# A spectral block beside a gated feed-forward: the sixteen-point stages as 64x64 matmuls, filter loads on GpSimd's queue, roots moved up

## The chip, the core and the metric

The kernel runs on one core of a Trainium2 chip. The metric is the time of one execution on the device in microseconds; the time before is the median of three runs. A profiled execution gives the trace: what each engine (TensorE, VectorE, ScalarE, GpSimd, and SyncE, which issues DMAs) did, and what it waited for. PE in the profile is TensorE, PEld its weight loads, DVE VectorE, ACT ScalarE, POOL GpSimd, SP SyncE, and SPq the queue on which SyncE issues DMAs.

## What is computed

The input is 2048 rows of 640 values in bf16. Cut to what matters, the reference is:

```python
xn = _layernorm(x, axis=-1)                      # 2048 x 640
X  = jnp.fft.rfft2(xn, axes=(-2, -1))            # 2048 x 321 complex
s  = jnp.fft.irfft2(X * (w_r + 1j * w_i), s=(S, D), axes=(-2, -1))
g  = _silu((_gelu(xn @ w_gate) * (xn @ w_up)) @ w_down)   # 640 -> 1536 -> 640
return x + s * g
```

So two independent branches start from the normalized input: a two-dimensional Fourier filter, and a feed-forward part with two input matrices of 640 x 1536 and one output matrix of 1536 x 640. Their product is added to the input.

## The kernel before

**Tiling.** The 2048 rows are 16 slabs of 128 rows (row = 16 n2 + n1, a slab is one n1). The feed-forward part works on four groups g of four slabs, 512 rows each: for each of 12 tiles t of the hidden dimension five matmuls into `psg` and five into `psu` (L634), GELU on ScalarE into `ge` (L638), the product into `uT` on VectorE (L640), then the down matmuls (L650) and the gate (`gate_out`).

**The Fourier branch.** The transform over 2048 rows is split into 128 x 16. Stage 1 (`slab_S1`, `slab_D`) does the 128-point part and the transform over the 640 columns, slab by slab, and stores the result in the DRAM scratch `ZDR`. After all 16 slabs `load_B2` reads it back with the 16-point direction on partitions: partition = (real or imaginary, n1, a), with 32 further row indices h in the free dimension (`B2`, 128 x 32 x 321). The sixteen-point stage `pair_S2(h)` handles two of these 32 indices: two matmuls of 128 x 128 by 128 x 321 with the weights `MG` into `px`, a copy to `xs` on ScalarE, and two products `p1`, `p2` with the filters `W1`, `W2` on VectorE. `pair_S2i(h)` is the inverse: four matmuls with `N1`, `N2` into `pu`, a copy to `us`, and two stores into the DRAM scratch `UDR`. The filter's partitions hold pairs of 16-point sets, so that `MG`, `N1` and `N2` are 128 x 128 with zeros where the sets don't mix (the mask `mk`, L333). Then `load_V` reads `UDR`, `vfold`, `slab_S1i` and `slab_Di` make the output of the branch, and `multiply_add` joins it with the gate and stores.

**The order.** Nothing is scheduled by a planner. The list `back` holds 144 slots of feed-forward work in order, one slot being five matmuls of 512 columns, ten of 256, or eight down matmuls (1.08 to 1.09 us each). `put(s, ...)` attaches other work to slot s, and the build issues each slot's feed-forward work and then its attached items. Each engine executes its own instructions in that order, so an instruction that waits holds up all that is behind it on its engine. Group 0 of the feed-forward part ends at slot 35, group 1 at 71, group 2 at 107.

**Where the touched steps stand.** The filter loads (`w_plus`, `w_minus`, `w_dup`) are issued by SyncE, one item behind each early `slab_D`; `w_edge` halves two columns on GpSimd at slots 50 and 53. The tables for the 16-point stage are made by `mg_iota`, `mg_phase` (GpSimd, slot 14), `mg_wrap` (VectorE, slot 20), `mg_sin` (ScalarE, slot 22), `mg_build` (58) and `mg_turn` (61). Statistics of a slab (`stats`) are followed, some slots later, by the inverse square roots of a group (`rsqrt4_a`, `rsqrt4_b`, which end in `nb`), then by `norm` on VectorE and `norm_act` on ScalarE (L430). `tfwd(1)`, slot 27, fills the second half of the table `Tfwd` on ScalarE (L232). `load_B2` is at slot 58. The pairs run from slot 66:

```python
    sb = z_end + 8
    for h in range(NS):
        down = back[sb][0] is down_third
        put(sb, pair_S2, h)
        if h > 0:
            put(sb + (0 if down else 1), pair_S2i, h - 1)
        sb += 1 if down else 2
    put(sb, pair_S2i, NS - 1)
    put(sb, load_V)
    vs0 = sb + 9
```

This gives slots 66 to 92, `load_V` at 92 and the first `slab_S1i` at 101. PSUM is split into two banks each for `psg` and `psu`, and two buffers of two banks each (`psB`) for all the rest, `px` and `pu` among it.

Of the kernel before, what the change touches and what calls it, by code (L numbers as in the profile page):

```python
# [14 lines left out]
P = 128  # L15
# [60 lines left out]
def build(nc, env):  # L76
# [26 lines left out]

    def w_plus(i, lo):
        WT, sp = spw[i]
        for ri in range(2):
            p0 = ri * 64 + lo * 16
            nc.sync.dma_start(out=WT[p0:p0 + 16, :, :], in_=sp[:, lo * 32:lo * 32 + 32, :])

    def w_minus(i, lo):  # L110
        WT, sp = spw[i]
        if lo == 0:
            nc.sync.dma_start(out=WT[32:48, :, :], in_=sp[:, 96:64:-1, :])
        else:
            nc.sync.dma_start(out=WT[48:64, 1:NH, :], in_=sp[:, 127:96:-1, :])
            nc.sync.dma_start(out=WT[48:64, 0, :], in_=sp[:, 64, :])

    def w_dup(i):
        WT = spw[i][0]
        nc.sync.dma_start(out=WT[96:128, :, :], in_=WT[32:64, :, :])  # L120
# [10 lines left out]
    MG = consts.tile([P, 2, P], BF16)  # L131
# [87 lines left out]
    def tinv_row():  # L219
        row = consts.tile([1, P], BF16)  # L220
        nc.gpsimd.memset(row[:, 0:P:2], 1.0)
        nc.gpsimd.memset(row[:, 1:P:2], -1.0)
        nc.sync.dma_start(out=Tinv[64:65], in_=row.unsqueeze(1).to_broadcast([1, NS, P]))
# [56 lines left out]
    def mg_iota():  # L280
        kr = mtile([2, 2, 2, 16], INT32, "kr")
        lc = mtile([2, 2, 2, 16], INT32, "lc")
        for ri in range(2):
            nc.gpsimd.iota(kr[:, ri, 0], pattern=[[0, 2], [1, 16]], base=0, channel_multiplier=0)
            nc.gpsimd.iota(kr[:, ri, 1], pattern=[[0, 2], [-1, 16]], base=15, channel_multiplier=0)
            nc.gpsimd.iota(lc[:, ri, 0], pattern=[[1, 2], [0, 16]], base=0, channel_multiplier=0)
            nc.gpsimd.iota(lc[:, ri, 1], pattern=[[-1, 2], [0, 16]], base=1, channel_multiplier=0)
        mg["kr"], mg["lc"] = kr, lc

    def mg_phase():  # L290
        n1_f, z_f = bits("mb", [(2, 15), (1, 1)])
        mg["z"] = z_f
        kr = mg["kr"]

        def aff(name, src, a, b):
            t = c1(name)
            nc.gpsimd.tensor_scalar(out=t, in0=src, scalar1=float(a), scalar2=b, op0=ALU.mult, op1=ALU.add)
            return t

        n1x = aff("n1x", n1_f, 128.0, 0.0)  # L300
        zc = aff("zc", z_f, -512.0, 512.0 + 1024.0)
        php0 = aff("php0", hi_f, 512.0, zc)
        php1 = aff("php1", php0, 1.0, 512.0)
        phm0 = aff("phm0", hi_f, -512.0, zc)
        phm1 = aff("phm1", phm0, 1.0, 1536.0)
        phs0 = aff("phs0", hi_f, 512.0, 1536.0)
        phs1 = aff("phs1", phs0, 1.0, 512.0)
        phs2 = aff("phs2", n1_f, 64.0, phs0)
        phs3 = aff("phs3", phs2, 1.0, 512.0)
        vg = mtile([2, 2, 2, 16], INT32, "vg")  # L310
        vs = mtile([4, 16], INT32, "vs")
        for ri, pm, ph in ((0, 0, php0), (1, 0, php1), (0, 1, phm0), (1, 1, phm1)):
            nc.gpsimd.tensor_scalar(out=vg[:, ri, pm], in0=kr[:, ri, pm], scalar1=n1x, scalar2=ph,
                                    op0=ALU.mult, op1=ALU.add)
        for j, ph in enumerate((phs0, phs1, phs2, phs3)):
            nc.gpsimd.tensor_scalar(out=vs[:, j, :], in0=kr[:, 0, 0, 0, :], scalar1=n1x, scalar2=ph,
                                    op0=ALU.mult, op1=ALU.add)
        mg["vgf"], mg["vs"] = vg.rearrange("p a b c d -> p (a b c d)"), vs
# [5 lines left out]
    def mg_sin():  # L324
        mg["sg"] = sg = mtile([P], FP32, "sg")
        mg["ss"] = ss = mtile([4, 16], FP32, "ss")
        nc.scalar.activation(out=sg, in_=mg["vgf"], func=ACT.Sin, bias=negpi, scale=TWO_PI / 2048.0)
        nc.scalar.activation(out=ss, in_=mg["vs"], func=ACT.Sin, bias=negpi, scale=TWO_PI / 2048.0)

    def mg_build():  # L330
        sg, ss, z_f, lo_f = mg["sg"], mg["ss"], mg["z"], lo_b
        mk = mg["kr"].rearrange("p a b c d -> p (a b c d)").bitcast(FP32)
        nc.vector.tensor_scalar(out=mk, in0=mg["lc"].rearrange("p a b c d -> p (a b c d)"), scalar1=lo_f,  # L333
                                scalar2=None, op0=ALU.is_equal)
        nc.vector.tensor_tensor(out=MG[:, 1, :], in0=sg, in1=mk, op=ALU.mult)
        nc.vector.tensor_copy(out=MG[:, 0, :], in_=MG[:, 1, :])
        lo0 = affine("lo0", lo_f, -1.0, 1.0)
        mz1 = c1("mz1")
        nc.vector.tensor_tensor(out=mz1, in0=z_f, in1=lo0, op=ALU.mult)
        mz0 = c1("mz0")  # L340
        nc.vector.tensor_tensor(out=mz0, in0=lo0, in1=mz1, op=ALU.subtract)
        for ri in range(2):
            for pm, mz in ((0, mz0), (1, mz1)):
                q0 = ri * 64 + pm * 32 + pm * 16
                nc.vector.tensor_scalar(out=MG[:, 0, q0:q0 + 16], in0=ss[:, pm * 2 + ri, :], scalar1=mz,
                                        scalar2=None, op0=ALU.mult)
        mg["MJ"] = MJ = mtile([2, P], BF16, "MJ")
        nc.vector.tensor_copy(out=MJ[:, :, 0:64], in_=MG[:, :, 64:128])
        nc.vector.tensor_scalar_mul(out=MJ[:, :, 64:128], in0=MG[:, :, 0:64], scalar1=-1.0)

    def mg_turn():
        MJ = mg["MJ"]
        pt = psB.tile([P, 4, P], BF16, tag="b")
        for k in range(2):
            nc.tensor.transpose(out=pt[:, k, :], in_=MG[:, k, :], identity=ident)
            nc.tensor.transpose(out=pt[:, 2 + k, :], in_=MJ[:, k, :], identity=ident)
# [160 lines left out]
    def load_B2():  # L517
        B2 = big.tile([P, NH, L], BF16, tag="sB", name="B2")
        zv = ZDR.rearrange("c n (a h) l -> (c n a) h l", a=4)
        for q in range(4):  # L520
            nc.sync.dma_start(out=B2[:, 8 * q:8 * q + 8, :], in_=zv[:, 8 * q:8 * q + 8, :])
        st_b["B2"] = B2

    def pair_S2(h):
        B2 = st_b["B2"]
        px = psB.tile([P, 2, 512], FP32, tag="b")
        for k in range(2):
            hi = 2 * h + k
            nc.tensor.matmul(px[:, k, 0:L], lhsT=MG[:, min(hi, 1), :], rhs=B2[:, hi, :], start=True, stop=True)  # L529
        xs = work.tile([P, 2 * L], BF16, tag="m1", bufs=2)  # L530
        nc.scalar.copy(out=xs.rearrange("p (k l) -> p k l", k=2), in_=px[:, :, 0:L])  # L531
        p1 = work.tile([P, 2 * L], BF16, tag="p1", bufs=2)
        p2 = work.tile([P, 2 * L], BF16, tag="p2", bufs=2)
        for pp, WT in ((p1, W1), (p2, W2)):
            nc.vector.tensor_tensor(out=pp, in0=xs, in1=WT[:, 2 * h:2 * h + 2, :].rearrange("p k l -> p (k l)"),  # L535
                                    op=ALU.mult)
        st_b[h] = (p1, p2)

    uv = UDR.rearrange("n (a h) f -> (n a) h f", a=4)

    def pair_S2i(h):
        p1, p2 = st_b.pop(h)
        pu = psB.tile([P, 2, 512], FP32, tag="b")
        for NM, pp, first in ((N1, p1, True), (N2, p2, False)):
            for k in range(2):
                hi = 2 * h + k
                nc.tensor.matmul(pu[:, k, 0:L], lhsT=NM[:, min(hi, 1), :], rhs=pp[:, k * L:(k + 1) * L],  # L547
                                 start=first, stop=not first)
        us = work.tile([P, 2, L], BF16, tag="m2", bufs=3)
        nc.scalar.copy(out=us, in_=pu[:, :, 0:L])  # L550
        nc.sync.dma_start(out=uv[:, 2 * h:2 * h + 2, 0:L], in_=us[0:64, :, :])
        nc.sync.dma_start(out=uv[:, 2 * h:2 * h + 2, L:D], in_=us[64:128, :, 1:320])
# [3 lines left out]
    def load_V():  # L556
        V = big.tile([P, NS, D], BF16, tag="sB", name="Vin")
        for g in range(4):
            nc.sync.dma_start(out=V[:, 4 * g:4 * g + 4, :],
                              in_=UDR.rearrange("n p f -> p n f")[:, 4 * g:4 * g + 4, :])  # L560
# [30 lines left out]
    def slab_Di(n1):  # L591
        py = psB.tile([P, 2, 512], FP32, tag="b")
        d_matmuls(py, st_c.pop(n1))
        eo = work.tile([P, 2, LP], BF16, tag="p1", bufs=2)
# [32 lines left out]
    def ffn_piece(g, t, k, c0, c1_):  # L627
# [8 lines left out]
        if k == 0:  # L636
            cur["ge"] = work.tile([P, 512], BF16, tag="ge", bufs=3, name="ge")[:, c0:c1_]
            nc.scalar.activation(out=cur["ge"], in_=ps, func=ACT.Gelu_apprx_tanh)  # L638
        else:
            nc.vector.tensor_tensor(out=uT[g][:, t, c0:c1_], in0=ps, in1=cur["ge"], op=ALU.mult)  # L640

    def ffn_part(g, t, h):
        for k in range(2):
            ffn_piece(g, t, k, h * 256, h * 256 + 256)

# [87 lines left out]
    for g, st, rs, nf in ((1, (9, 10, 11, 12), 13, ((14, 15), (16, 17))), (2, (18, 20, 22, 24), 26, ((27, 28), (30, 32))),  # L733
                          (3, (33, 35, 37, 39), 40, ((41, 42), (45, 46)))):
# [18 lines left out]
    for n1, item in enumerate(filt):  # L753
        put([sl for sl, it in f_units.items() if it == (slab_D, n1)][0], *item)
    put(50, w_edge, 0)
    put(53, w_edge, 1)
    put(2, vt_iota, 1)
    put(12, tinv_angle, 1)
# [12 lines left out]
    for h in range(NS):  # L771
        down = back[sb][0] is down_third
        put(sb, pair_S2, h)
        if h > 0:
            put(sb + (0 if down else 1), pair_S2i, h - 1)
        sb += 1 if down else 2
    put(sb, pair_S2i, NS - 1)
    put(sb, load_V)
    vs0 = sb + 9
# [35 lines left out]
    for s, b in enumerate(back):  # L815
        b[0](*b[1:])
        for it in plan[s]:
            it[0](*it[1:])
    assert len(left) == 0
# [30 lines left out]
```

## Time and profile before

| | |
|---|---|
| median of 3 runs (lowest to highest) | 218.66 us (217.79 to 218.76) |
| the profiled execution's own time | 218.46 us |
| its span (first to last instruction) | 216.3 us |
| instructions | 4227 |
| TensorE busy | 203.4 us, 94% of the span |
| VectorE, ScalarE, GpSimd busy | 144.0, 129.3, 14.4 us |
| DMA moved | 31.77 MB in 35253 packets |

Lines in the profile read as follows. A group of instructions: line, engine, operation, output <- inputs, shape, count | busy us in all, mean ns of one | idle us of the engine just before them and what ended it. A wait: who <- for whom, us in all, times, longest. A piece of the chain: start us, length us, engine and what. A row of the timeline: start us, length us, engine, line, operation, what, and in brackets the idle time just before it and what ended it. Matmuls are pipelined: one's length in the profile is longer than the distance to the next one's start. All times are of one execution, counted from the span's start.

### The profile page before, as it was taken

Reading aid. Unit: us, or ns where it says so; the run is one execution under the profiler, and the core shown is the slowest. Engines: PE = TensorE matmul, PEld = TensorE weight load, DVE = VectorE, ACT = ScalarE, POOL = GpSimd, SP = SyncE. Lnnn points to the kernel's source line nnn. Section 1 sums busy time; section 2 is a strip of 40 time slices with the busy share of each in tenths; the row PEclk is TensorE's granted clock in tenths of the full one; section 3 lists DMA queues with packets and bytes.
Section 4 is the critical chain, followed back from the end, with each engine's and each line's share of the span. In section 5 each row is a group of like instructions: output and inputs, shape, how many; then the busy total and the mean of one; then the engine's idle time right before and its main releaser. Section 6 shows DMA issues by size and latency. Waiting matters only on the chain.

```text
span 216.3 us, 4227 instructions
## 1 busy us (share of the span) xinstructions
PE 203.4 (94%) x1504; PEld 131.8 (61%) x1504; DVE 144.0 (67%) x478; ACT 129.3 (60%) x215; POOL 14.4 (7%) x44
## 2 busy tenths in 40 slices
PE   0699999998999999999999999999999999999993
PEld 0389984676665555567665555557676656666773
DVE  8888988956987852352665544543667888894442
ACT  7556567594764945533785656651467666765721
POOL 8000203800000000000000000000000000000000
PEclk9999999999999999999999999999999999999999
DMA  5999999999999996329542222233943433322131
GB/s 163 344 363 361 340 161 105 142 149 134 128 203 212 159 210 112 75 62 334 185 91 62 62 58 48 47 79 102 371 150 95 120 121 100 112 66 64 28 108 50
DMA packets 35253, 31.77 MB, mean 147 GB/s; under 512 B 10336, under 2 KB 34016, under 8 KB 35040
## 3 DMA queue, kind: packets, MB, share of 16 engines
q1 hardware_dynamic: 35232, 31.50, 64.1%
q8 instruction: 12, 0.20, 0.4%
q14 instruction: 9, 0.07, 0.1%
HBM read 20.34 MB, written 7.87 MB: 130 GB/s over the span
## 4 chain that ended last, share of the span: by engine, by line
PE 81%; DVE 6%; ACT 5%; DMA 5%; issue 1%; SPq 0%; ACTq 0%; DVEq 0%
PE psg L634 22%; PE psu L634 22%; PE psg L650 9%; PE psu L650 9%; PE pu L547 4%; PE pv L583 2%; PE py L503 2%; PE py L502 2%; PE px L529 2%; DMA Vin<-UDR 2%; PE pd L502 2%; PE pd L503 2%; PE pz L494 2%; DMA UDR<-us 2%; PE pw L273 1%
## 5 line engine op out<-in xcount | busy, mean ns | idle before, releaser
L634 PE MATMUL psg<-xnT,Wg 128*128 128x512 bf16 (+1 forms) x275 | 61.4, 354 | 0.0
L634 PE MATMUL psu<-xnT,Wu 128*128 128x512 bf16 (+1 forms) x275 | 60.9, 352 | 0.0
L650 PEld LDWEIGHTS <-uT 128*128 128x128 bf16 x396 | 37.5, 98 | 13.7 <-DVE uT L640 0.2
L640 DVE TENSOR_TENSOR uT<-psu,ge 128x512 bf16<-128x512 f32 (+1 forms) x55 | 33.9, 616 | 17.4 <-PE psu L634 17.0
L638 ACT ACTIVATE ge<-psg 128x512 bf16<-128x512 f32 (+1 forms) x55 | 29.9, 544 | 19.1 <-PE psg L634 16.9
L634 PEld LDWEIGHTS <-Wg 128*128 128x128 bf16 x275 | 25.9, 99 | 18.4 <-issue 0.6
L634 PEld LDWEIGHTS <-Wu 128*128 128x128 bf16 x275 | 26.3, 98 | 17.8
L650 PE MATMUL psg<-Wd,uT 128*128 128x320 bf16 (+1 forms) x204 | 30.8, 295 | 0.0
L650 PE MATMUL psu<-Wd,uT 128*128 128x320 bf16 (+1 forms) x192 | 29.0, 295 | 0.0
L535 DVE TENSOR_TENSOR p<-xs,W 128x642 bf16<-128x642 bf16 x32 | 14.4, 492 | 17.5 <-ACT xs L531 17.3
L585 ACT CAST vs<-pv 128x640 bf16<-128x640 f32 x16 | 11.1, 692 | 9.6 <-PE pv L583 9.6
L550 ACT CAST us<-pu 128x642 bf16<-128x642 f32 x16 | 11.2, 698 | 7.4 <-PE pu L547 7.4
L512 ACT CAST zd<-pd 128x644 bf16<-128x644 f32 x16 | 11.1, 694 | 6.0 <-PE pd L503 4.0
L373 DVE BATCH_NORM_STATS2 st<-X 128x6 f32<-128x320 bf16 x32 | 13.9, 477 | 0.0
L496 ACT CAST Z<-pz 128x640 bf16<-128x640 f32 x16 | 11.0, 689 | 4.0 <-PE pz L494 4.0
L607 DVE TENSOR_TENSOR Yall<-Yall,G 128x640 bf16<-128x640 bf16 (+2 forms) x21 | 8.7, 412 | 6.2 <-ACT G L686 5.8
L595 ACT ACTIVATE eo<-py 128x644 bf16<-128x644 f32 x16 | 11.3, 707 | 1.8 <-PE py L503 1.5
L531 ACT CAST xs<-px 128x642 bf16<-128x642 f32 x16 | 11.0, 690 | 2.2 <-PE px L529 1.3
L502 PE MATMUL pd<-FT,Z 128*128 128x161 bf16 x64 | 10.4, 233 | 1.4 <-ACT Tfwd L232 1.4
L547 PE MATMUL pu<-p,N 128*128 128x321 bf16 x64 | 11.6, 301 | 0.0
L681 DVE SCALAR_TENSOR_TENSOR G<-th,psg 128x320 bf16<-128x320 f32 x12 | 5.8, 481 | 7.1 <-ACT th L680 7.1
L502 PE MATMUL py<-FT,vs 128*128 128x161 bf16 x64 | 10.5, 233 | 0.0
(150 smaller groups left out, 242.6 us busy)
## 6 DMA issues: line engine op xcount, KB each, us to landing
ZDR<-zd SPq DMA_DIRECT2D x16, 160.5 KB, 6.2
B<-ZDR SPq DMA_DIRECT2D x4, 642.0 KB, 6.1
Vin<-UDR SPq DMA_DIRECT2D x4, 640.0 KB, 6.3
xt<-in_A_x_dram SPq DMA_DIRECT2D x16, 160.0 KB, 2.5
Wg<-in_B_w_gate_dram SPq DMA_DIRECT2D x4, 480.0 KB, 7.5
Wu<-in_B_w_up_dram SPq DMA_DIRECT2D x4, 480.0 KB, 8.5
X<-in_A_x_dram SPq DMA_DIRECT2D x3, 640.0 KB, 9.0
Wd<-in_B_w_down_dram SPq DMA_DIRECT2D x1, 1920.0 KB, 13.9
```

The costliest lines, as they stand in the source:

```text
L373: nc.vector.bn_stats(out=st[:, k, :], in_=xr[:, k, :])
L502: nc.tensor.matmul(o, lhsT=lhs[:, 2 * b + k, :], rhs=FT[:, 2 * b + k, :], start=True, stop=False)
L512: nc.scalar.copy(out=zd.rearrange("p c (m b) -> p c m b", b=2), in_=natural(pd))
L535: nc.vector.tensor_tensor(out=pp, in0=xs, in1=WT[:, 2 * h:2 * h + 2, :].rearrange("p k l -> p (k l)"), op=ALU.mult)
L547: nc.tensor.matmul(pu[:, k, 0:L], lhsT=NM[:, min(hi, 1), :], rhs=pp[:, k * L:(k + 1) * L], start=first, stop=not first)
L550: nc.scalar.copy(out=us, in_=pu[:, :, 0:L])
L585: nc.scalar.copy(out=vs, in_=pv)
L595: nc.scalar.activation(out=eo.rearrange("p c (m b) -> p c m b", b=2), in_=natural(py), func=ACT.Copy, scale=(2.0 if n1 >= 12 else 1.0) / ( ...
L634: nc.tensor.matmul(ps, lhsT=WT[:, c, t * P:(t + 1) * P], rhs=xnT[g][:, c, c0:c1_], start=(c == 0), stop=(c == 4))
L638: nc.scalar.activation(out=cur["ge"], in_=ps, func=ACT.Gelu_apprx_tanh)
L640: nc.vector.tensor_tensor(out=uT[g][:, t, c0:c1_], in0=ps, in1=cur["ge"], op=ALU.mult)
L650: nc.tensor.matmul(ph, lhsT=uT[g][:, t, j * P:(j + 1) * P], rhs=Wd[:, t, c0:c1_], start=(t == 0), stop=(t == NT - 1))
```

## The change

The diff has three parts. First, the sixteen-point stage: `B2`, the filters and `UDR` are laid out so that the 128 partitions are two halves of 64, `MG` shrinks from 128 x 128 with zeros to 64 columns, and `pair_S2` becomes `quad_S2`: four matmuls, each with 64 rows and 64 columns of weights, from the lower or upper 64 partitions into the lower or upper 64 partitions of `px`. `quad_S2i` has eight such matmuls and four stores of 32 partitions in place of four matmuls and two stores of 64. The inverse follows two quads behind and `p1`, `p2` get a third buffer; two quads go in three slots (66, 67, 69, 70, 72, ...), `load_V` is at slot 91, its first load is split in two, and the first `slab_S1i` is at 102. In the slots with a quad, GELU is issued behind the quad's copies (`late`, `flush`). Second, all filter loads are issued by GpSimd, in smaller pieces (38 instead of 16), from slot 13 on; nine of them come before `mg_phase` in GpSimd's order. The two memsets of `row_fill` go up to slot 11. Third, the roots of groups 1, 2 and 3 move from slots 13, 26, 40 to 12, 24, 39, right behind the last statistics of the group.

```diff
     def w_plus(i, lo):
         WT, sp = spw[i]
-        for ri in range(2):
-            p0 = ri * 64 + lo * 16
-            nc.sync.dma_start(out=WT[p0:p0 + 16, :, :], in_=sp[:, lo * 32:lo * 32 + 32, :])
+        src = halves(sp[:, lo * 32:lo * 32 + 32, :])
+        for half in range(2):
+            for ri in range(2):
+                nc.gpsimd.dma_start(out=w_rows(WT, half * 64 + ri * 32, lo), in_=src[:, half])
 
     def w_minus(i, lo):
         WT, sp = spw[i]
+        for half in range(2):
+            for b in range(2):
+                s0 = 1 if lo == half == b == 0 else 0
+                r = 128 - lo * 32 - b * 16 - half * 8
+                q = lo * 16 + b * 8
+                nc.gpsimd.dma_start(out=WT[half * 64 + 16:half * 64 + 32, q + s0:q + 8, :],
+                                  in_=sp[:, r - s0:r - 8:-1, :])
         if lo == 0:
-            nc.sync.dma_start(out=WT[32:48, :, :], in_=sp[:, 96:64:-1, :])
-        else:
-            nc.sync.dma_start(out=WT[48:64, 1:NH, :], in_=sp[:, 127:96:-1, :])
-            nc.sync.dma_start(out=WT[48:64, 0, :], in_=sp[:, 64, :])
+            nc.gpsimd.dma_start(out=WT[16:32, 0, :], in_=sp[:, 64, :])
...
-    MG = consts.tile([P, 2, P], BF16)
+    MG = consts.tile([P, 3, 64], BF16)
...
-        zv = ZDR.rearrange("c n (a h) l -> (c n a) h l", a=4)
+        B2 = big.tile([P, 2, 2, 8, L], BF16, tag="sB", name="B2")
+        zv = ZDR.rearrange("c n (z lo b h s) l -> lo (c n z) b h s l", z=2, lo=2, b=2, h=2)
         for q in range(4):
-            nc.sync.dma_start(out=B2[:, 8 * q:8 * q + 8, :], in_=zv[:, 8 * q:8 * q + 8, :])
+            b, s = q // 2, q % 2 * 4
+            for lo in range(2):
+                nc.sync.dma_start(out=B2[lo * 64:lo * 64 + 64, b, :, s:s + 4, :], in_=zv[lo][:, b, :, s:s + 4, :])
...
-    def pair_S2(h):
+    def quad_S2(j):
         B2 = st_b["B2"]
         px = psB.tile([P, 2, 512], FP32, tag="b")
-        for k in range(2):
-            hi = 2 * h + k
-            nc.tensor.matmul(px[:, k, 0:L], lhsT=MG[:, min(hi, 1), :], rhs=B2[:, hi, :], start=True, stop=True)
...
+        for lo in range(2):
+            rows = slice(lo * 64, lo * 64 + 64)
+            for half in range(2):
+                nc.tensor.matmul(px[half * 64:half * 64 + 64, lo, 0:L], lhsT=MG[rows, min(j + half, 1), :],
+                                 rhs=B2[rows, j // 8, half, j % 8, :], start=True, stop=True)
+        xs = work.tile([P, 2, L], BF16, tag="m1", bufs=2)
+        nc.scalar.copy(out=xs, in_=px[:, :, 0:L])
+        p1 = work.tile([P, 2, L], BF16, tag="p1", bufs=3)
+        p2 = work.tile([P, 2, L], BF16, tag="p2", bufs=3)
         for pp, WT in ((p1, W1), (p2, W2)):
...
+            nc.vector.tensor_tensor(out=pp, in0=xs, in1=WT[:, j:j + 17:16, :], op=ALU.mult)
...
+    def quad_S2i(j):
+        p1, p2 = st_b.pop(j)
         pu = psB.tile([P, 2, 512], FP32, tag="b")
         for NM, pp, first in ((N1, p1, True), (N2, p2, False)):
...
+            for half in range(2):
+                rows = slice(half * 64, half * 64 + 64)
+                for lo in range(2):
+                    cols = slice(lo * 64, lo * 64 + 64)
+                    nc.tensor.matmul(pu[cols, half, 0:L], lhsT=NM[rows, min(j, 1), cols], rhs=pp[rows, lo, :],
+                                     start=first, stop=not first)
         us = work.tile([P, 2, L], BF16, tag="m2", bufs=3)
         nc.scalar.copy(out=us, in_=pu[:, :, 0:L])
-        nc.sync.dma_start(out=uv[:, 2 * h:2 * h + 2, 0:L], in_=us[0:64, :, :])
-        nc.sync.dma_start(out=uv[:, 2 * h:2 * h + 2, L:D], in_=us[64:128, :, 1:320])
+        for lo in range(2):
+            to = uv[lo][:, j // 8, :, j % 8, :]
+            nc.sync.dma_start(out=to[:, :, 0:L], in_=us[lo * 64:lo * 64 + 32, :, :])
+            nc.sync.dma_start(out=to[:, :, L:D], in_=us[lo * 64 + 32:lo * 64 + 64, :, 1:320])
...
-    for g, st, rs, nf in ((1, (9, 10, 11, 12), 13, ((14, 15), (16, 17))), (2, (18, 20, 22, 24), 26, ((27, 28), (30, 32))),
-                          (3, (33, 35, 37, 39), 40, ((41, 42), (45, 46)))):
+    for g, st, rs, nf in ((1, (9, 10, 11, 12), 12, ((14, 15), (16, 17))), (2, (18, 20, 22, 24), 24, ((27, 28), (30, 32))),
+                          (3, (33, 35, 37, 39), 39, ((41, 42), (45, 46)))):
...
-    for n1, item in enumerate(filt):
-        put([sl for sl, it in f_units.items() if it == (slab_D, n1)][0], *item)
+    for k, item in enumerate(filt):
+        put(13 if k < 2 else 15 + k, *item)
...
-    for h in range(NS):
-        down = back[sb][0] is down_third
-        put(sb, pair_S2, h)
-        if h > 0:
-            put(sb + (0 if down else 1), pair_S2i, h - 1)
-        sb += 1 if down else 2
-    put(sb, pair_S2i, NS - 1)
+    for j in range(NS):
+        put(sb, quad_S2, j)
+        if j > 1:
+            put(sb, quad_S2i, j - 2)
+        sb += 2 if sb % 3 == 1 else 1
+    put(sb, quad_S2i, NS - 2)
+    put(sb + 1, quad_S2i, NS - 1)
+    sb += 1
     put(sb, load_V)
-    vs0 = sb + 9
+    vs0 = sb + 11
...
         b[0](*b[1:])
+        if not any(it[0] is quad_S2 for it in plan[s]):
+            flush()
         for it in plan[s]:
             it[0](*it[1:])
+        flush()
```

## The prediction

> **What bounds the kernel now.** I read the page's busy rows first, then what each engine waited for, then the chain that ended last, then the timelines around the edits.
>
> ```profile
> PE 203.4 (94%) x1504; PEld 131.8 (61%) x1504; DVE 144.0 (67%) x478; ACT 129.3 (60%) x215; POOL 14.4 (7%) x44
> ...
> PE   0699999998999999999999999999999999999993
> ...
> PEclk9999999999999999999999999999999999999999
> ```
>
> TensorE is busy from the second slice to the end, at the full granted clock. The list of TensorE's waits says how little is left to stalls:
>
> ```profile
> PE pw L273 <- ACT Tinv L217: 7.4, 1, 7.4
> PE pd L502 <- ACT Tfwd L232: 1.4, 1, 1.4
> PE pv L583 <- DVE f L443: 0.2, 1, 0.2
> PE pz L494 <- DVE f L443: 0.2, 1, 0.2
> ```
>
> The first wait is the start-up, which the change leaves alone. The second, 1.4 us, can be removed. Beyond these, time can only come from matmul time itself. The chain that ended last prices it:
>
> ```profile
> 15.27 0.45 PE pt L231 x8
> ...
> 111.84 1.08 PE psg L634 x5
> 112.92 0.28 PE px L529 x2
> 113.19 1.08 PE psu L634 x5
> 114.27 0.55 PE pu L547 x4
> ```
>
> Here `px` (two matmuls) and `pu` (four) stand bare on the chain between feed-forward matmuls: 0.27 + 0.55 = 0.82 us per pair, 16 pairs, 13.1 us in all, 0.136 us per matmul of 321 columns. The groups by line give the length of one instruction:
>
> ```profile
> L547 PE MATMUL pu<-p,N 128*128 128x321 bf16 x64 | 11.6, 301 | 0.0
> ...
> L529 PE MATMUL px<-B,MG 128*128 128x321 bf16 x32 | 7.0, 301 | 0.0
> ...
> L547 PEld LDWEIGHTS <-N 128*128 128x128 bf16 x64 | 6.3, 98 | 4.6 <-issue 0.4
> ```
>
> A matmul lasts 301 ns but the next starts 136 ns later: 165 ns of each is overlapped by its successor.
>
> **64x64 matmuls.** The kernel had 32 + 64 = 96 matmuls here; the changed one has 4 + 8 = 12 per quad, 192. The gain exists only if four on different quarters of the array run at once: three sets per quad. Upper bound of the gain: 3 x 0.136 = 0.41 us per quad, 0.41 x 16 = 6.5 us gained. Upper bound of the loss: no overlap, 12 x 0.136 = 1.63 us, 13.0 us lost. No instruction of before works on part of the array, so the value must come from neighbours. The load of weights: the eight 128-column transposes above, each with its own load, take 0.45 us, 56 ns per load and matmul, so four come to 0.22 us if loads and starts are the limit, and 0.136 us if the streaming is. The 98 ns loads before 161-column matmuls leave those at 70 ns each, pure streaming, so loads hide well; I take 0.16 us a set, 0.48 us a quad. Then the change between whole-array and quarter-array work, into and out of each of 18 slots: nothing at the least, and the 165 ns overlap twice at the most, 0.33 us per slot. I take half, 0.165. A quad is then 0.645 us against 0.82: 0.175 x 16 = 2.8 us gained, all on the chain.
>
> The Trainium skill speaks against this edit: "TensorEngine Tiling (Array Packing)", Key Properties, says that a change of tiling mode drains the TensorE, and its Restrictions say that column tiling switches off fast weight load. No instruction in this trace shows either. By that rule the switch counts in full: 0.48 + 0.33 = 0.81 us a quad, nothing gained from this edit, and a total some 2.8 us above mine.
>
> **Inverse two behind, GELU late, three buffers of p.** `pu` of quad j-2 finds its products made one or two slots ago; the 0.3 us that the first pair lost is gone. ScalarE has, per three slots, 2 x (0.69 + 0.70) of copies and 1.5 x 0.60 of GELU, 3.7 us in about 4.5. GELU comes up to 1.3 us later; psg and psu have two banks each, so the matmuls after it do not wait; without that cover each would lose 0.6 us. VectorE's products keep 642 elements; rows now start on odd elements, but L599 does that too (319 elements, 321 ns against 327 for 321): nothing.
>
> **Filter loads on GpSimd.** 16 loads leave SP and 38 smaller ones go on GpSimd, nine of them ahead of `mg_phase`. The timelines of GpSimd, VectorE and ScalarE:
>
> ```profile
> 24.67 1.20 POOL L207 TENSOR_SCALAR GEN<-GEN,pb,ph_t 128x1024 int32<-128x1024 int32 x1
> 35.33 0.19 POOL L297 TENSOR_SCALAR n1x<-mb 128x1 f32<-128x1 f32 x1 [9.45 <-DVE mb L184]
> ...
> 40.74 1.90 POOL L316 TENSOR_SCALAR vs<-kr,n1x,phs 128x16 int32<-128x16 int32 x4
> ```
>
> ```profile
> 43.04 0.17 DVE L322 TENSOR_SCALAR vg<-vg 128x128 int32<-128x128 int32 x1
> ...
> 48.97 0.49 DVE L681 SCALAR_TENSOR_TENSOR G<-th,psg 128x320 bf16<-128x320 f32 x1 [2.42 <-ACT th L680]
> ```
>
> GpSimd idles 9.45 us until `mb`; nine issues must fit there, 1.05 us each. What is behind: `mg_phase`, then `mg_wrap` on VectorE (0.4 us of slack), and behind that `uT`, whose last piece TensorE takes at once. No issue of GpSimd is in the trace. Bounds from rows: 0.46 us, SP's for a filter load, to 1.20 us, GpSimd's longest operation: 4.1 to 10.8 us, so 0 to 1.35 - 0.45 = 0.9 us of stall. A gain is excluded, since `mb` sets the start anyway. I take 0.4. The other 29 come after `mg_phase` with nothing behind them but the two edge multiplies, at 29 x 1.2 = 35 us still 20 us ahead of the first quad. SP's queue gets emptier, but TensorE never waited for it.
>
> The skill's "DMA: Bandwidth & Descriptors", SWDGE vs HWDGE vs iDMA, says that GpSimd writes such descriptors itself into SBUF, and that VectorE's two-port modes lock it out meanwhile. If every issue were held so, the nine would not fit and the total would rise by whatever passes 9.45 us. No run here shows it.
>
> **Roots behind statistics.** ScalarE's timeline:
>
> ```profile
> 52.67 0.92 ACT L430 ACTIVATE X<-X,nb,nrn 128x640 bf16<-128x640 bf16 x1 [2.80 <-DVE nb L424]
> 53.50 0.99 ACT L232 COPY Tfwd<-pt 128x1024 bf16<-128x1024 bf16 x1
> ```
>
> The `Tfwd` copy that TensorE waits 1.4 us for stands behind L430, which waits for the roots. The 2.3 us of roots now fill the 2.42 us that VectorE idles before 48.97. L430 then starts near 49.9 and `Tfwd` is done near 51.8, where TensorE needs it at 53.1: 1.4 us gained. What is late next is the matmuls themselves. In the first group the roots go ahead of one `uT`, which then ends about 2.3 us later, with its second psu bank as cover until 34.2 us: nothing.
>
> **SP's stores and loads.** Each quad has four stores of 32 partitions instead of two of 64:
>
> ```profile
> 110.77 0.57 SPq L551 DMA_DIRECT2D UDR<-us  x1
> 111.39 0.61 SPq L552 DMA_DIRECT2D UDR<-us  x1
> ```
>
> From start to start 0.62 us. Three slots bring two quads, eight stores; TensorE needs 3 x 1.08 + 2 x 0.645 = 4.53 us for them, so 0.566 us a store is the limit. Rows on either side: 0.62 for 64 partitions, 0.50 for the filter's 16 (0.46 plus a gap). At 0.62 SP falls behind by 0.43 us in three slots, 3.0 us over seven rounds; the three `us` buffers cover about 1.4 (three quads last 6.8; copy, issue and landing take 0.7 + 2.5 + 2.2), so 0 to 1.6 us. I take the middle of the rows, 0.56, just inside, and 0.4 us. The load of B is eight issues for four, the first quad waiting for two: up to 0.4 us (0.34 to 0.42 each) against some 0.5 of slack: 0.1. V is loaded 11 slots ahead instead of 9, two slots (2.2 us) against two more stores (1.2 us), so the 0.2 us wait of `pv` goes.
>
> **Sum.** -2.8 - 1.4 - 0.2 + 0.4 (GpSimd) + 0.4 (stores) + 0.1 (B) = -3.5. The profiled execution took 218.46 us, its span 216.3 and 2.2 around it, within 0.1% of the runs' median of 218.66. Forecast: 218.46 - 3.5 = 215.0.
>
> **Rivals.** (a) Full overlap, free switches: -6.5 for -2.8. SP's stores at 0.50 then just keep up (4.0 us against 4.06); at 0.56 they give 1.5 back. 210.9 to 212.4. For it: loads hide well elsewhere. (b) SP sets the pace: at 0.62 us a store the 60 stores before the last quad take 37.2 us whatever TensorE saves; what remains is the roots' 1.4 and little else, 217.0. For it: the 64-partition rows; against it: the 16-partition ones. (c) Slower: quarter matmuls run only two abreast and both switches cost in full: 6 x 0.136 + 0.33 = 1.15 us a quad in `quad_S2` and `quad_S2i`, 0.33 x 16 = +5.2, less 1.4, so 222.3. It decides from 0.91 us a quad, where the roots' gain is used up. For it: the trace has no partial-array instruction, and 301 against 136 ns shows how much overlap a switch could break. (d) GpSimd late: at 1.5 us an issue the nine take 13.5, 3.6 us of stall: 218.2; at 2 us 222.7.
>
> **How the numbers follow.** Forecast 0.40 (213 to 217.5), (a) 0.12, (b) 0.14, (c) 0.22, (d) 0.12. Range 210.8 to 221.8: it leaves out the upper part of (c) and (d), and a little of (a). No change is within 0.5%, 217.57 to 219.75, about what a measurement of this kernel can tell. Faster: 0.38 + 0.12 + 0.08 + 0 + 0.03 = 0.61; same: 0.02 + 0 + 0.05 + 0.02 + 0.03 = 0.12; slower: 0.01 + 0.20 + 0.06 = 0.27.
>
> **What would show it.** Right: `px` and `pu` at 0.6 to 0.7 us a quad on the chain, the L502 wait on `Tfwd` gone, `n1x` still at about 35.3 us. Wrong: `px` or `pu` matmuls one after another; TensorE or ScalarE waiting for the U stores; `vg` on VectorE waiting for GpSimd. A quad above 0.91 us, or `n1x` after 38 us, overturns the sign.

## The result and the profile after

The changed kernel takes 231.65 us (median of four runs) against 218.5 in the same rounds: a ratio of 1.058, interval 1.047 to 1.069. The forecast was 215.0. Medians are over all runs, ratios leave out runs over 1.5% above the same kernel's fastest, and the profiled execution here, 235.88 us with a span of 234.1, is such a run; the other three spans are 228.2 to 231.5. Three rows of the page, busy tenths in 40 slices of 5.85 us:

```profile
PE   0799999999991001999999999999999999999993
...
PEclk9999999999999555899999999999999999999999
DMA  6999999899996899811179423233592343331131
```

Before, both upper rows were nines but for the ends and one slice. Now the digits 1001 of TensorE's row, from 71 to 93 us, are a standstill, and the granted clock falls with it. The DMA row is mostly full in that time: transfers run, but not the one that is waited for. The lists of waits of TensorE and of ScalarE (who <- for whom: us in all, times, longest):

```profile
PE pd L509 <- ACT zd L519: 21.7, 1, 21.7
PE pw L289 <- ACT Tinv L230: 7.1, 1, 7.1
PE px L539 <- DMA B<-ZDR: 0.5, 1, 0.5
...
ACT zd L519 <- DMA ZDR<-zd: 23.1, 2, 22.9
```

It is one wait. `zd` is the tile with a slab's finished rows. It has three buffers, and ScalarE may not write the next slab into one until its store to `ZDR` has landed. TensorE's D stage waits for ScalarE, and all later matmuls stand behind that. The chain that ended last names the store, and the timeline of SP shows when it was issued:

```profile
59.00 33.17 DMA ZDR<-zd
```

```profile
49.25 9.66 SPq L491 DMA_TRANSPOSE xnT<-X  x4
59.00 14.88 SPq L520 DMA_DIRECT2D ZDR<-zd  x3
73.99 0.72 SPq L239 DMA_DIRECT2D Tinv<-row  x1
74.80 16.55 SPq L491 DMA_TRANSPOSE xnT<-X  x2
```

The tile was ready at 52.96 us; its store was issued at 59.00, behind four transposes of `xnT` in SP's order, and landed 33.17 us later. Before, a store of `ZDR` took 6.2 us to land (median; 10.2 at most), a transpose 10.0 at most, and now up to 36.3. The queues, and the filter's transfers that have moved to GpSimd's:

```profile
q1 hardware_dynamic: 33840, 26.25, 47.5%
q0 software_dynamic: 1696, 5.26, 19.3%
```

```profile
W<-in_A_w_r_dram POOLq DMA_DIRECT2D x8, 160.5 KB, 9.0
W<-W POOLq DMA_DIRECT2D x4, 321.0 KB, 24.5
W<-in_A_w_i_dram POOLq DMA_DIRECT2D x8, 160.5 KB, 20.2
```

GpSimd's queue carries 1696 packets to SP's 33840, but 19.3% of the engines' time. The four copies inside SBUF (`w_dup`) land after 24.5 us; before, two of twice the size took 6.7. The trace's single packets say the same: one of the copies' rows of 20544 bytes took 3.95 us on average, against 2.06 for all rows of that length before. From 63 to 81 us, SP's transposes moved 516 packets of 256 bytes; before, 2154 went through from 60 to 63 us alone.

The matmuls did what was forecast. The groups, and the timeline of TensorE:

```profile
L559 PE MATMUL pu<-p,N 64*64 64x321 bf16 x128 | 7.2, 300 | 0.0
L539 PE MATMUL px<-B,MG 64*64 64x321 bf16 x64 | 5.6, 321 | 0.5 <-DMA B<-ZDR 0.5
```

```profile
126.65 0.33 PE L539 MATMUL px<-B,MG 64*64 64x321 bf16 x4
126.81 0.45 PE L559 MATMUL pu<-p,N 64*64 64x321 bf16 x8
127.19 0.72 PE L673 MATMUL psg<-Wd,uT 128*128 128x320 bf16 x4
127.75 0.71 PE L673 MATMUL psu<-Wd,uT 128*128 128x320 bf16 x4
128.38 0.33 PE L539 MATMUL px<-B,MG 64*64 64x321 bf16 x4
```

From one quad to the next 1.73 us, of which eight down matmuls take 1.09: 0.64 us a quad. Four quarter matmuls do run at once.

Span against span, 234.1 - 216.3 = 17.8 us. The wait is +21.7, the lower clock just behind it about +1.4 (below), the wait for `B` +0.5, the quads -2.9, the `Tfwd` wait -1.4, two short waits for `f` -0.4: +18.9, one more than measured.

### The profile page after: what moved, and what is told of

Read it like the earlier page. It is cut to its first block, busy times and chain, and to the rows that moved or that the text cites. A ratio compares the mean times of both kernels' runs of the same rounds, so it can differ in the third digit from the quotient of the medians.

```text
span 234.1 us, 4482 instructions
## 1 busy us (share of the span) xinstructions
PE 199.7 (85%) x1582; PEld 125.9 (54%) x1600; DVE 144.3 (62%) x475; ACT 127.5 (54%) x215; POOL 33.7 (14%) x78
## 3 DMA queue, kind: packets, MB, share of 16 engines
q1 hardware_dynamic: 33840, 26.25, 47.5%
q0 software_dynamic: 1696, 5.26, 19.3%
## 4 chain that ended last, share of the span: by engine, by line
PE 75%; DMA 17%; DVE 2%; ACT 2%; issue 1%; SPq 0%; POOL 0%; POOLq 0%; ACTq 0%
PE psg L649 20%; PE psu L649 19%; DMA ZDR<-zd 15%; PE psg L673 10%; PE psu L673 10%; DMA B<-ZDR 2%; PE pu L559 2%; PE pv L598 2%; PE py L510 2%; PE py L509 2%; PE px L539 2%; PE pd L509 2%; PE pd L510 2%; PE pz L501 2%; PE pw L289 1%
## 5 line engine op out<-in xcount | busy, mean ns | idle before, releaser
L649 PE MATMUL psg<-xnT,Wg 128*128 128x512 bf16 (+1 forms) x263 | 60.2, 355 | 0.8 <-issue 0.3
L649 PE MATMUL psu<-xnT,Wu 128*128 128x512 bf16 (+1 forms) x269 | 59.9, 351 | 0.4 <-issue 0.3
L649 PEld LDWEIGHTS <-Wu 128*128 128x128 bf16 x275 | 25.5, 98 | 19.6 <-issue 2.1
L509 PE MATMUL pd<-FT,Z 128*128 128x161 bf16 x64 | 10.9, 239 | 21.7 <-ACT zd L519 21.7
L546 DVE TENSOR_TENSOR p<-xs,W 128x642 bf16<-128x642 bf16 x32 | 14.4, 493 | 10.2 <-ACT xs L542 10.1
L510 PEld LDWEIGHTS <-Z 128*128 128x128 bf16 x64 | 6.4, 100 | 23.4 <-issue 22.0
L510 PE MATMUL pd<-TR,Z 128*128 128x161 bf16 x64 | 10.9, 240 | 0.0
```

What stands on the lines that cost most here:

```text
L509: nc.tensor.matmul(o, lhsT=lhs[:, 2 * b + k, :], rhs=FT[:, 2 * b + k, :], start=True, stop=False)
L510: nc.tensor.matmul(o, lhsT=lhs[:, 4, :], rhs=TR[:, b, k, :], start=False, stop=True)
L546: nc.vector.tensor_tensor(out=pp, in0=xs, in1=WT[:, j:j + 17:16, :], op=ALU.mult)
L649: nc.tensor.matmul(ps, lhsT=WT[:, c, t * P:(t + 1) * P], rhs=xnT[g][:, c, c0:c1_], start=(c == 0), stop=(c == 4))
```

## The experiments

**First round: queue, place or kind of the transfers; the roots alone.** Theory Q: two queues share the engines, and the large packets of GpSimd's hold up SP's small ones. Rivals: the pieces or their dense place cost on any queue; the copies cost by their kind.

`e1_sp`: all 38 loads and copies on SP, in the same slots.

```diff
-                nc.gpsimd.dma_start(out=w_rows(...), in_=src[:, half])
+                nc.sync.dma_start(out=w_rows(...), in_=src[:, half])
```

> The changed kernel with its 38 filter loads issued by SP instead of GpSimd, at the same slots. Theory Q (a second queue takes the DMA engines away from SP's queue, so that one ZDR store lands 33 us late): the 21.7 us wait of TensorE is gone, the store lands in under 12 us, and the time is that of the quads and roots alone, 214 to 217 us. Theory L (the smaller pieces and the copies between partitions are slow whoever issues them): a ZDR store still lands over 20 us late and the time stays at 225 us or more. Either way SP has some 22 more issues of 0.5 us; up to 3 us of waits of ScalarE for ZDR buffers may come of that.

Measured: 230.37 us, 1.054 (1.050 to 1.058). TensorE waits 12.2 us for `zd`. The stall has another form here, as SP's timeline shows:

```profile
61.51 10.92 SPq L115 DMA_DIRECT2D W<-in_A_w_i_dram  x8
73.45 0.38 SPq L520 DMA_DIRECT2D ZDR<-zd  x1
```

SP spends 10.92 us on eight loads in a row, and the store is issued only behind them. No store takes more than 11.5 us to land here, so neither theory holds as written: the second queue's long landings are gone, and the time is not back. Packed this densely, the loads may not stand in SP's order either.

`e2_before_gp`: the kernel before, with its 16 loads and copies issued by GpSimd.

> The kernel before with its 16 filter loads issued by GpSimd instead of SP, in their old pieces and slots. Theory Q: a ZDR store lands over 20 us late and TensorE waits for it, 222 us or more. Theory L: no such wait, 217 to 219.5 us. GpSimd's order changes too: mg_phase stands behind the first loads, which costs under 1 us by the 0.5 us that an issue took.

Measured: 240.49 us, 1.101 (1.095 to 1.106). The move alone, without any other part of the change, costs 22 us. Its two copies and eight of its loads have rows of 20.5 KB, and SP needs 35.8 us to issue one group of four transposes.

`e3_nodup`: the changed kernel, the copies replaced by 18 more reversed loads from DRAM, still on GpSimd.

```diff
-            nc.gpsimd.dma_start(out=WT[p0 + 32:p0 + 48, :, :], in_=WT[p0:p0 + 16, :, :])
+        w_minus(i, 0, 48)
+        w_minus(i, 1, 48)
```

> The changed kernel with its four copies W<-W (rows of 20.5 KB, which took up to 9.9 us a packet) replaced by 18 more reversed loads from DRAM, still on GpSimd. Theory D (the copies between partitions hold the DMA engines): the long wait is gone or under 5 us, 214 to 219 us. Theory Q without D: the wait stays, over 10 us, 225 us or more, since the bytes on GpSimd's queue are the same.

Measured: 220.20 us, 1.007 (1.004 to 1.010); the wait for `zd` is 6.6 us. So some 11 of the 13 us lost go with the copies.

`e4_roots`: the kernel before, with only the roots moved (slots 13, 26, 40 to 12, 24, 39).

> The kernel before with only the roots moved up by one or two slots. By the prediction's step: TensorE's 1.4 us wait for the Tfwd copy goes and the time falls by 1.4 us, ratio 0.9936. If the wait is only handed on to the next buffer or to VectorE's later uT, it falls by less than 0.5 us.

Measured: 218.07 us, 1.001 (0.998 to 1.003). The wait for `Tfwd` is gone and nothing is gained; TensorE's list has a new line:

```profile
PE pd L502 <- ACT zd L512: 1.2, 1, 1.2
```

**Second round: where the items stand.** In the kernel before, one item of the loads stands behind each D stage, slots 10 to 42; the change packs them into 13 to 24.

```diff
-    for k, item in enumerate(filt):
-        put(13 if k < 2 else 15 + k, *item)
+    for n1, item in enumerate(filt):
+        put([sl for sl, it in f_units.items() if it == (slab_D, n1)][0], *item)
```

> The changed kernel with all its filter loads and copies issued by SP again, and one item of them behind each slab's D stage (slots 10 to 42) as in the kernel before; sixteen-point stage, roots and the rest as changed. Theory 1 (the sixteen-point stages brought what the prediction said, and the whole loss comes from the loads being issued densely on a queue of their own): the 21.7 us wait of L509 is gone, ratio about 0.985 to 0.99 (215.2 to 216.5 us: 16 quads at 0.17 us less each, the roots worth nothing). Theory 2 (the finer pieces of the changed layout, 5 KB instead of 20 KB rows, cost by themselves on any queue): a wait for a ZDR store of some us stays, ratio 1.00 to 1.02.

> As e5_sp_spread, with the four SBUF to SBUF copies of W replaced by 18 more reversed loads from DRAM. Theory 1 (copies hurt only where they meet other transfers in a dense stretch): same as e5_sp_spread within 0.5%. Theory 2 (copies of 20 KB rows hold up the stores behind them wherever they stand): 1 us or more faster than e5_sp_spread.

> The changed kernel with its loads on GpSimd, copies included, but one item behind each D stage (slots 10 to 42) instead of packed into slots 13 to 24. Theory A (density: ten items in 12 slots collide with the xnT transposes and the ZDR stores): the stall goes, ratio 0.985 to 0.995. Theory B (a second queue with 20 KB packets starves SP's small packets wherever it stands): a wait of 10 us or more for a ZDR store stays, ratio 1.04 or more.

> As e7_gp_spread, with the four copies replaced by 18 more reversed loads from DRAM. Theory A (density): 0.985 to 0.99, as e5 and e6. Theory B (the copies' 20 KB packets): the same as theory A here, but with e7 at 1.04 or more. Theory C (any second queue costs some us, whatever its packets): 1.00 to 1.01, as the packed version of it (1.0066).

Measured: e5 217.26 us, 0.993 (0.990 to 0.997); e6 218.57, 1.001 (0.999 to 1.003); e7 235.49, 1.079 (1.077 to 1.082); e8 223.35, 1.024 (1.019 to 1.030). On SP, spreading is worth 13 us (e1 to e5). On GpSimd's queue it is worth nothing, and both versions are 3 to 4 us slower; density is not the cause there. The copies cost 12 us on GpSimd's queue (e7 against e8) and nothing on SP's, where the version without them is 1.3 us slower. So kind alone is not it, but kind and queue together. e5 is the first version ahead of the kernel before, but by 1.1 us of the 3.5 forecast; in its profiled execution (219.41 us) TensorE waits 3.7 us for `zd`.

**Third round: buffers, row length, order on SP.** `e9_sp_bufs` is e5, and `e10_after_bufs` the changed kernel, with a fourth buffer (the same edit stands at `us`, which shares the tile):

```diff
-        zd = work.tile([P, 2, LP], BF16, tag="m2", bufs=3)
+        zd = work.tile([P, 2, LP], BF16, tag="m2", bufs=4)
```

> As e5_sp_spread, with four buffers instead of three for the tile that zd and us share. Theory 1 (what keeps e5 from the forecast is the 3.7 us wait for a zd buffer): that wait goes, ratio 0.975 to 0.985 (213 to 215 us). Theory 2 (SP issues the stores too late, behind 38 loads, so that a fourth buffer only moves the wait to the load of B): ratio as e5, 0.99 to 1.00.

> The changed kernel as it is (loads and copies on GpSimd), with four buffers for the tile of zd and us. Theory 1 (the buffers are too few for a late store): the wait of L509 falls from 21.7 to under 10 us, time under 222 us. Theory 2 (the transfers are starved, and the buffer is only where it shows): wait of L509 15 to 20 us, or the same sum with the wait for B, time 226 to 231 us.

Measured: e9 216.87 us, 0.992 (0.989 to 0.994), the wait of `pd` gone; e10 234.56 us in a single run, wait 18.8. In the changed kernel a fourth buffer gives back 3 us of wait and, as far as one run can say, no time (the changed kernel's runs are 230.0 to 235.88): the transfers are late, and the buffer is only where it shows. In e9 the wait did not go, it moved to the first quad, `px`, which waits 2.3 us for `B`, in two pieces of 1.21 and 1.14. And it costs twice. The windows of e9 (us, then busy time of PE, PEld, DVE, ACT, POOL, granted clock, DMA share, GB/s):

```profile
100.00:103.00 3.00, 0.69 (x5) 0.32 (x6) 0.00 (x0) 0.00 (x1) 0.00 (x0) 1.00 1.07 229
103.00:106.00 3.00, 3.00 (x17) 1.48 (x17) 1.60 (x4) 1.78 (x3) 0.00 (x0) 0.61 1.05 223
106.00:109.00 3.00, 3.00 (x27) 1.70 (x26) 1.08 (x3) 0.81 (x2) 0.00 (x0) 0.82 1.09 231
```

After 2.3 idle us, TensorE gets 0.61 and 0.82 of its clock for the next six: (0.39 + 0.18) x 3 = 1.7 us more.

`e11_dup_quarters`: the changed kernel with each copy cut into four, so that a row is 5.1 KB long.

```diff
-            nc.gpsimd.dma_start(out=WT[p0 + 32:p0 + 48, :, :], in_=WT[p0:p0 + 16, :, :])
+            for q in range(0, NH, 8):
+                nc.gpsimd.dma_start(out=WT[p0 + 32:p0 + 48, q:q + 8, :], in_=WT[p0:p0 + 16, q:q + 8, :])
```

> The changed kernel with each of the four copies of W cut into four of 80 KB: rows of 5.1 KB instead of 20.5 KB, as the loads have; still on GpSimd and still SBUF to SBUF. Theory 1 (the long rows are what starves SP's small packets): as e3_nodup, 219 to 223 us, wait of L509 5 to 8 us. Theory 2 (the kind of transfer, or its waits in GpSimd's order): 228 us or more, wait of L509 15 us or more.

Measured: 222.76 us in a single run. Waits of TensorE, and the landing of the copies:

```profile
PE pd L510 <- ACT zd L520: 7.1, 1, 7.1
```

```profile
W<-W POOLq DMA_DIRECT2D x16, 80.2 KB, 8.9
```

Same bytes, same partitions, same queue, four times as many issues, and 9 us under the changed kernel's median, 7 under its fastest run. So not the kind of transfer, but the length of the rows, or the size of an issue, which shrinks with it from 321 to 80 KB; no run separates these two.

`e13_sp_late`: e9 with the last two items at slots 47 and 49, behind SP's last transposes, and the second edge multiply at 60.

> As e9_sp_bufs, with the last two items (the plus half of W2, eight loads) moved from slots 39 and 42 to slots 47 and 49, behind SP's last transposes, and the edge multiply of W2 from slot 53 to 60. Theory 1 (eight loads in front of transposes and stores in SP's order hold up the Z stage): 1 to 2 us faster than e9, 212 to 214 us. Theory 2 (the transfer time of the DMA engines up to the load of B is what counts, in whatever order): as e9 within 0.5%.

Measured: 216.94 us, 0.991 (0.987 to 0.995), the same as e9. No wait of TensorE for `zd`, and 3.4 us for `B` (issued from 96.44 us; the first quad starts at 100.82), with the lower clock behind it: the wait has moved on once more.

**Fourth round: the rest of the forecast's gain, and the roots again.** `e14_sp_b_later`: e13 with `sb = z_end + 11` for `+ 8`, three more slots of matmuls between the load of `B` and the first quad.

> As e13_sp_late, with the sixteen-point stage three slots later, so that three more slots of feed-forward matmuls stand between the load of B and the first quad. Theory 1 (what is left to the forecast is the wait for B, 3.4 us in e13, and the lower clock behind it): both go, 213 to 215.5 us, ratio 0.975 to 0.986. Theory 2 (the wait only moves on, to the load of V or to the end, which is now three slots nearer): 216.5 us or more.

Measured: 212.95 us, 0.974 (0.970 to 0.978), the fastest version of all, 5.3 us under the kernel before. Its clock and its waits:

```profile
PEclk9999999999999999999999999999999999999999
```

```profile
PE pw L289 <- ACT Tinv L230: 7.0, 1, 7.0
PE px L539 <- DMA B<-ZDR: 1.5, 2, 1.1
```

`e12_before_roots_bufs` (roots moved, four buffers) and its control `e16_before_bufs` (four buffers alone), both from the kernel before:

> The kernel before with the roots right behind the statistics and four buffers for the tile of zd and us. Theory 1 (the roots take 1.4 us of wait away, and in e4_roots a wait for a zd buffer took its place): 216.5 to 217.5 us, at least 1 us under e16_before_bufs or e4_roots. Theory 2 (the stage's end is set by the transfers, whatever TensorE waits for in between): 218 us or more, as e4_roots, with the wait at the load of B.

> The kernel before with four buffers for the tile of zd and us and nothing else: the control for e12. Both theories: 218 to 219 us, no change, since TensorE waits for no zd buffer there.

Measured: e12 216.43 us, 0.993 (0.991 to 0.995); e16 218.25, 1.000 (0.998 to 1.002). The buffer alone is worth nothing, the roots alone nothing, both together 1.9 us.

`e15_act_store`: the changed kernel with the `ZDR` stores issued by ScalarE (`nc.scalar.dma_start`), so that they are not in SP's order.

> The changed kernel as it is (loads and copies on GpSimd), with the ZDR stores issued by ScalarE, so that they stand in another ring than SP's transposes. Theory 1 (a store is late because SP's ring hands its packets over in order, behind transposes that the long rows hold up): the wait of L509 falls below 8 us, time 218 to 224 us. Theory 2 (every ring's packets have to wait for engines that the long rows hold): wait of L509 12 us or more, time 226 us or more.

Measured: 224.86 us in a single run, between the two theories. The waits, and SP's timeline:

```profile
PE pd L509 <- ACT zd L519: 8.5, 1, 8.5
```

```profile
50.52 19.67 SPq L491 DMA_TRANSPOSE xnT<-X  x4
70.29 2.62 SPq L239 DMA_DIRECT2D Tinv<-row  x1
73.01 16.87 SPq L491 DMA_TRANSPOSE xnT<-X  x4
```

SP is stuck in its transposes even longer. The store that ScalarE waits for here was ready at 53.97 us, issued at 54.00, and landed at 79.30: 25.3 us, with no transpose ahead of it in its own order. In the changed kernel it was 39.2 us from ready to landed. Taken from these two executions, SP's order made some 14 us of these, 6 of them before the store was issued. The rest, 25.3 us, is still some 19 over a usual landing (6.2), in another queue than the transposes; that it is spent in waiting for the engines is a reading.

**Last: is GpSimd's queue usable?** `e17_gp_short` is e14 with loads and copies on GpSimd, the copies in quarters; `e18_gp_long` is e17 with the copies whole, and no other difference.

> As e14_sp_b_later (four buffers, sixteen-point stage three slots later, last two items at slots 47 and 49), with loads and copies issued by GpSimd again and each copy cut into four, so that no row on GpSimd's queue is over 5.1 KB. Theory 1 (only the long rows did the harm): as e14 within 1%, 212 to 215 us. Theory 2 (a second queue costs SP's packets turns whatever its rows): 216 us or more, with a wait for a zd buffer or for B of 2 us or more.

> As e17_gp_short, with the four copies whole again: rows of 20.5 KB on GpSimd's queue, in the arrangement that was good for short ones. Theory 1 (long rows on the second queue do the harm, wherever they stand): 6 us or more slower than e17, 220 us or more, and a wait of TensorE of 5 us or more behind a late ZDR store. Theory 2 (the buffers and the later stage were the cure, not the short rows): as e17 within 1%.

Measured: e17 214.49 us, 0.980 (0.976 to 0.984); e18 228.99, 1.050 (1.044 to 1.057). In e18:

```profile
PE pd L509 <- ACT zd L519: 12.3, 1, 12.3
```

```profile
50.67 21.11 SPq L491 DMA_TRANSPOSE xnT<-X  x4
```

The same four transposes take 8.48 us to issue in e17. Whether four copies, 1.3 of the 31.8 MB that the kernel moves, go in rows of 20.5 or of 5.1 KB decides over 14.5 us, even with four buffers and the later stage. With rows of 5.1 KB the second queue stands 0.6% above SP's (e17 against e14), but the intervals overlap, so that no cost is shown.

## Why the prediction was wrong

**The step that failed** is in the part on the filter loads: "29 come after `mg_phase` with nothing behind them but the two edge multiplies" and "SP's queue gets emptier, but TensorE never waited for it". Both look at GpSimd's and SP's orders alone. The bytes that left SP's queue did not leave the 16 engines that serve both. There, while GpSimd's loads and long copies moved, SP's transposes and stores hardly advanced, and SP's order was stuck: the store that TensorE waited 21.7 us for landed 39.2 us after its tile was ready. I had asked what waits for the loads, and not what the loads hold up. The wait was also in sight: `zd` has three buffers, and the list of before has ScalarE waiting 2.0 us for a store of `ZDR`, which I passed over because TensorE did not wait:

```profile
ACT zd L512 <- DMA ZDR<-zd: 2.0, 1, 2.0
```

The term was priced at 0 and cost 14 to 22 us: e18 against e17, e2 against before.

A rule that bears on this is in the Trainium skill, "DMA: Bandwidth & Descriptors", Queues, rings and completion order: each DMA engine goes round the queues it has work for, a whole packet at a time, before it turns to the next. Row length as the deciding quantity fits that. The turns themselves no run here shows, and row length alone is not the whole mechanism: in e18 SP's packets crawl before the long rows and after them too (last section). That rows of 20.5 KB do no such harm within SP's own queue I read from its order: in e14 the four transposes stand ahead of the copies and are through when these start.

**The quads: right.** Forecast 0.645 us a quad, measured 0.64, so 16 x 0.18 = 2.9 us. The terms held too: `px`, one set of four, takes 0.16 us to the start of `pu`; the two sets of `pu` with the way out take 0.38. At the way in, the first weight load starts after 0.26 us idle, so there is a price of changing, but inside the 0.64. That the sum came out so exactly is in part luck: 0.16 a set and half of 0.33 for the change were choices inside wide bounds, and 16 changes were charged for 18 slots, 0.3 us too few. The rule from the Trainium skill's "TensorEngine Tiling (Array Packing)", Key Properties, that a change of tiling mode drains the TensorE, would by the prediction's estimate have made 0.81, and the measurement decides against that size. Rivals (a), 0.41 us, and (c), two abreast, are out. On the whole kernel the gain shows once little else is late: e14 is 3.5 us under e12 by the medians. The profiled executions are 1.8 us apart (spans 212.0 and 213.8), where 2.9 for the quads, 0.2 for the wait of `pv` and 0.4 at the start-up stand against 1.5 of wait for `B` in e14.

**The roots: right about the wait, wrong about the time.** "What is late next is the matmuls themselves" failed: next was the store of `zd`, 1.2 us of TensorE's time in e4. With a fourth buffer the roots give 1.9 us, somewhat more than the 1.4.

**GpSimd's issues: harmless, but not by the reckoning.** An issue takes 0.54 us, half of the 1.05 that I allowed. But the ninth issue waits 4.53 us for a first load to land, which I had not reckoned with, and ends at 34.21 us, 0.51 after `mb` is ready (33.70). `n1x` starts right behind it, at 34.24 instead of 35.33, since `mb` too is earlier. I had priced 0.4 us, and no wait of TensorE came of it; rival (d) is out:

```profile
24.87 2.17 POOL L115 DMA_DIRECT2D W<-in_A_w_r_dram  x4
...
33.69 0.52 POOL L127 DMA_DIRECT2D W<-in_A_w_r_dram  x1 [4.53 <-DMA W<-in_A_w_r_dram]
34.24 0.43 POOL L311 TENSOR_SCALAR n1x<-mb 128x1 f32<-128x1 f32 x1
```

**The stores of U: cheaper than thought.** 32 partitions take 0.30 to 0.43 us to issue (three of the 64 take 1.3 to 1.6), 0.47 from start to start where they follow one another, under my bounds of 0.50 and 0.62, and nothing waits for them. Rival (b) is out; the 0.4 us were nothing.

**B: too small.** 0.1 us priced; 0.5 in the changed kernel, behind the long stall, and once the Z stage (`slab_S1` and `slab_D`) ran without stalls up to 3.4 us (e13), plus about 1.4 for the clock (0.84 and 0.59 in the windows from 100 and 103 us). **V: right**, the 0.2 us wait is gone.

With the loads back on SP, a fourth buffer and three slots, the terms nearly add up: 218.3 - 2.9 (quads) - 1.9 (roots with buffer) - 0.2 (V) + 1.5 (the wait for `B`) = 214.8. The profiled execution took 213.84, the median is 212.95, so that 1 to 2 us of the gain stay unaccounted for. None of the signs that the prediction listed as "wrong" occurred; the wait that decided was on no list.

## What to carry to other kernels

When transfers move to another queue, look at what they share with the transfers that stay: list who waits for those and how many buffers cover them, and compare the row lengths, since a few long rows on a second queue can hold up thousands of short ones on the first. Cut long contiguous rows before moving them. That alone is no licence: packed into slots 13 to 24, with three buffers, short rows on the second queue still left waits of 6.6 and 7.1 us (e3, e11). When a wait is taken away, find the next one in the list of the engine behind, and give it its buffer in the same change: here neither half was worth anything alone.

## What the runs showed of the hardware that was not expected

- The harm of long rows is not their own slowness. In e18 a row of 20.5 KB took 2.68 us on average, against 2.49 for the same copies on SP's queue in e14, and still e18 stalled for 12.3 us. In e14, too, few short packets pass while the long rows move: from 63 to 72 us none of 256 bytes and 256 of 642. But the four transposes stand ahead of them in SP's order and are through by then; they need 7.45 us to issue (from 53.15 us), and 21.11 in e18, beside GpSimd's queue.
- The long rows are not all of the jam. In e18 they run from 59.12 to 72.81 us, but SP's packets crawl before and after that, beside load rows of 5.1 KB on GpSimd's queue: from 54 to 60 us 149 transpose packets pass beside 128 such rows, from 72 to 84 us 650 beside 222. In e17 it is 1079 beside 112 and 1313 beside 208. So the long copies decide, but what keeps SP's queue slow in these stretches, no run shows.
- Four 64x64 matmuls of 321 columns run at once, a set in 0.16 us, though a single one lasts 0.30 us in the groups. Their weight loads take 103 to 106 ns, no less than 98 for a whole 128x128 one.
- A stall costs more than its length. In the changed kernel the clock was at 0.50 while TensorE stood, and only came back after work had resumed: 0.69 on average over 94 to 97 us. In e9 the two waits of 1.21 and 1.14 us were followed by 0.61 and 0.82. In e14, 0.38 and 1.14 us did not lower it.

The windows of the changed kernel, in the same columns as those of e9:

```profile
88.00:91.00 3.00, 0.00 (x0) 0.00 (x0) 0.00 (x0) 0.00 (x0) 0.00 (x0) 0.50 0.94 124
91.00:94.00 3.00, 1.00 (x8) 1.00 (x8) 0.52 (x1) 1.75 (x4) 0.00 (x0) 0.50 1.23 232
94.00:97.00 3.00, 3.00 (x11) 1.27 (x11) 2.55 (x9) 2.13 (x4) 0.58 (x1) 0.69 1.16 178
97.00:100.00 3.00, 2.95 (x24) 1.82 (x23) 0.69 (x1) 1.95 (x3) 0.00 (x0) 1.00 0.48 109
```

The 1.4 us of the sum above are from here: half of the busy 1.00 us at 0.50, and 0.31 x 3 at 0.69.
